# Attention and feed-forward on one core: weight sums behind the last split, PSUM quarters summed in place, Strassen from tile 8

## The chip, the cores and the metric

The kernel runs on one NeuronCore of a Trainium2 chip. The metric is the device time in microseconds of one execution; lower is better. The engines are TensorE (PE; its weight loads are shown apart as PEld), VectorE (DVE), ScalarE (ACT), GpSimd (POOL) and the queue that issues the DMAs (SP). Each works through its own instructions in order.

## What is computed

Sliding-window attention, plain for four heads and dilated by four for the other four, then a normalised feed-forward with a residual:

```python
x = attention(q, k, v)                      # B=8, H=8, S=576, D=64; window 32, dilation 4
x = x.transpose(0, 2, 1, 3).reshape(8, 576, 512)
mu, var = mean(x), mean((x - mu) ** 2)
xn = (x - mu) / sqrt(var + 1e-6) * g_ln
return x + maximum(xn @ w_ch1, 0) @ w_ch2   # w_ch1: 512 x 2048, w_ch2: 2048 x 512
```

The weights arrive as float64. Each float32 operand of a large product is split into two float16 halves, a high one (a rounded copy) and a low one (the rest), and a product is three products of halves: high x high, high x low, low x high.

## The kernel before

The 8 x 576 rows are 36 tiles of 128 rows. For each tile t the program records units of work: L (loads), S (scores), M (softmax), V (values), N (norm, and the halves for the transposes), T (two DMA transposes into xT). At the start stand the units of the weights: C and W (load and convert w1 and w2, L530 to L544), s and P (split into halves, L132 and L133). Every unit has a due time from a hand-written table (TIMES, and ORDER for the pairs); units are recorded by that time, and a scheduler then sets each engine's order by simulated durations, with the recording order as priority. `tc.high_priority()` lifts what stands under it; `tc.issue_after(i)` puts what stands under it behind instruction i.

The first FIRST tiles go through the feed-forward plainly: four up products of 512 columns a tile (`up_plain`, L344, 192 matmuls), the rectified halves (L351, L352), and a down product (`down_plain`, L363, 48 matmuls of 512 columns). All later tiles go in pairs of 256 rows through a Strassen scheme (Winograd's form): seven products where eight quarters would be multiplied. A half s (of two) of the feed-forward's columns takes seven up products (L418, 24 matmuls each) and seven down products (L487, 12 matmuls each), in the order 1, 5, 6, 2, 3, 7, 4 of their numbers. Product 1 starts the bank "u", to which 6, 7 and 4 add; 5 starts "f", to which 3 adds; 2 has "e". Between the additions `copied` takes a bank's state to SBUF (ACT L435). ORDER writes the sequence of a pair: "U06" is up product 6 of half 0, "D" a down product, "V1" and "S0" the next pair's attention, "N01" and "N05" the next pair's first two up products.

The four quarters of a half are A11, A12, A22 and A21; `added` sums a bank and a copy (DVE L440), rectifies (ACT L441), and `halves` makes a high half (ACT L426) and a low half (POOL L427). A21 is z21 (ACT L473). `summed` makes S1 = A21 + A22, S3 = A11 - A21, S2 = S1 - A11 and S4 = A12 - S2 on VectorE (L445), all operands in SBUF, and their halves. After a down product, `to_x` adds the bank into x (DVE L498); the next product into the same bank waits for it.

Strassen also needs sums of the weights, T1 to T4, for 2 weight matrices x 4 column groups: `combine` makes them in f32 (L390 to L397), then a high half (ACT L399) and a low half (L400). T1 and T2 are made on POOL, T3 and T4 on VectorE. T4 replaces a piece of the plain weights, so its halves are written after the last plain tile.

The pool z has 8 f32 buffers (NZ) for copies and sums, h has 12 for halves, ps_f has 6 PSUM banks; a buffer is given out in turn, and its next user waits until its last reader is done. The norm of a tile is: statistics (DVE L271, after the four DMAs x<-xd of L264), a power on POOL (L276), the normalised x (DVE L290), for a pair's second tile four sums (POOL L300), the halves (ACT L308, POOL L309), the transposes (L324).

Of the kernel before, what the change touches and what calls it, by code (L numbers as in the profile page):

```python
# [59 lines left out]
def attention_then_ffn(ctx: ExitStack, tc, qkv, masks, g, w1, w2, out):  # L60
    nc = tc.nc
# [68 lines left out]

    def split(src, scale, hi, lo):
        nc.scalar.activation(hi, src, AF.Copy, scale=scale)  # L132
        nc.vector.scalar_tensor_tensor(  # L133
            out=lo, in0=src, scalar=scale, in1=hi, op0=ALU.mult, op1=ALU.subtract
        )
# [247 lines left out]
    def combine(w, op, fg):  # L383
        sub, add = ALU.subtract, ALU.add
        x, y = {"T1": ("12", "11"), "T2": ("22", None), "T3": ("22", "12"), "T4": ("21", "T2")}[op]
        e = nc.vector if op in ("T3", "T4") else nc.gpsimd
        (xh, xl) = piece(w, x, fg)
        if y is None:
            z = state.pop(("T1", w, fg))
            e.tensor_tensor(out=z, in0=xh, in1=z, op=sub)  # L390
            e.tensor_tensor(out=z, in0=z, in1=xl, op=add)
        else:
            yh, yl = piece(w, y, fg)
            z = f32_tile().rearrange("p (c f) -> p c f", c=2)
            e.tensor_tensor(out=z, in0=xh, in1=yh, op=sub)
            e.tensor_tensor(out=z, in0=z, in1=xl, op=add)
            e.tensor_tensor(out=z, in0=z, in1=yl, op=sub)  # L397
        hi, lo = piece(w, op, fg)
        nc.scalar.copy(hi, z)  # L399
        e.tensor_tensor(out=lo, in0=z, in1=hi, op=sub)  # L400
        if op == "T1":
            state["T1", w, fg] = z
# [7 lines left out]
    def up_product(n, s, to, start):  # L410
        x, w = PRODUCTS[n]
        q = QUARTER[x]
        for j in range(HG):
            fc = slice(j % 2 * P, (j % 2 + 1) * P)
            ws = piece(0, w, 2 * s + j // 2)
            for k in range(2):
                for m, (l, r) in enumerate(triple([a[:, k, fc] for a in ws], (xT_pair[:, 0, q, k], xT_pair[:, 1, q, k]))):
                    nc.tensor.matmul(  # L418
                        to[:, j * P : (j + 1) * P], l, r, start=start and j == 0 and k == 0 and m == 0,
                        stop=j == HG - 1 and k == 1 and m == 2, skip_group_check=not start,  # L420
                    )

    def halves(name, me, z):
        h = me[name] = halves_tile()
        hh, hl = flat(h)
        nc.scalar.copy(hh, z)  # L426
        nc.gpsimd.tensor_tensor(out=hl, in0=z, in1=hh, op=ALU.subtract)  # L427

    def up(n, s, t0):
        me = state.setdefault(("s", t0, s), {})  # L430

        def copied(x):
            z = f32_tile()
            with tc.high_priority():
                nc.scalar.copy(z, x)  # L435
            return z

        def added(x, z, name):
            with tc.high_priority():
                nc.vector.tensor_tensor(out=z, in0=x, in1=z, op=ALU.add)  # L440
            nc.scalar.activation(z, z, AF.Relu)  # L441
            halves(name, me, z)

        def summed(to, x, y, op, name):
            nc.vector.tensor_tensor(out=me[to], in0=me[x], in1=me[y], op=op)  # L445
            halves(name, me, me[to])

        if n == 1:
            me["u"] = bank()
            up_product(1, s, me["u"], True)  # L450
            me["z11"] = copied(me["u"])
        elif n == 5:
            me["f"] = bank()
            up_product(5, s, me["f"], True)
            me["z22"] = copied(me["f"])
        elif n == 6:
            up_product(6, s, me["u"], False)
            me["z12"] = copied(me["u"])
        elif n == 2:
            e = bank()  # L460
            up_product(2, s, e, True)
            added(e, me["z11"], "A11")
        elif n == 3:
            up_product(3, s, me["f"], False)
            added(me["f"], me["z12"], "A12")
        elif n == 7:
            up_product(7, s, me["u"], False)
            added(me["u"], me["z22"], "A22")
        else:
            up_product(4, s, me["u"], False)  # L470
            me["z21"] = f32_tile()
            with tc.high_priority():
                nc.scalar.activation(me["z21"], me["u"], AF.Relu)  # L473
# [310 lines left out]
```

## Time and profile before

| | |
|---|---|
| median of 3 runs | 958.19 us (956.5 to 958.92) |
| profiled execution | 956.94 us, its span 955.1 us |
| busy share of the span: PE, DVE, POOL, ACT | 86%, 63%, 55%, 40% |
| weights arrive and are converted, first tiles | 0 to 132 us |
| plain tiles, from the first down product | 132 to 260.5 us |
| 15 pairs by Strassen | 260.5 to 955.1 us |
| mean granted TensorE clock | 0.973 of full speed |

A matmul is pipelined, so a busy PE is not PE at its peak. In the rows of the profile "out<-in" are the program's names, "x12" a count; a releaser is what ended an engine's idle time. w_sb are the weights' halves, w_sums the raw weights at first and T1 to T3 later.

### The profile page before, as it was taken

The numbers are of one execution on the slowest core, as the hardware profiler recorded it, in microseconds if no ns is written. First come the engines' busy times: TensorE is split into PE (matmuls) and PEld (weight loads), VectorE is DVE, ScalarE is ACT, GpSimd is POOL, SyncE is SP. The second block draws the span as 40 slices with busy tenths as digits, with TensorE's granted clock in tenths as the row PEclk, the third lists the DMA queues.
The fourth block names the chain that finished last, engine by engine and source line by source line (L and its number), as shares of the span: only waits on it lengthen the run. The fifth ranks groups of instructions, "written<-read, shape, count | busy, mean of one in ns | idle before, by whom it ended". The sixth has DMA issues, their size and how long they took to land.

```text
span 955.1 us, 36608 instructions
## 1 busy us (share of the span) xinstructions
PE 822.5 (86%) x16592; PEld 727.2 (76%) x16592; DVE 604.8 (63%) x1021; ACT 377.6 (40%) x624; POOL 522.1 (55%) x451
## 2 busy tenths in 40 slices
PE   3318799956999999989999899988999898898998
PEld 2218765753798988888988899887888798787897
DVE  5998663698655757474748383828473837374834
ACT  4343361220352625252534344434253425353442
POOL 2153055595356657474848483838283827374844
PEclk9999799977999999999999999999999999999999
DMA  9833523301323232323332323232324142322020
GB/s 335 301 104 132 80 65 89 69 29 34 96 75 84 78 79 77 91 62 95 80 84 71 96 58 96 58 96 57 107 46 96 45 108 58 77 66 57 19 52 24
DMA packets 118236, 81.84 MB, mean 86 GB/s; under 512 B 67840, under 2 KB 100160, under 8 KB 118080
## 3 DMA queue, kind: packets, MB, share of 16 engines
q1 hardware_dynamic: 118080, 79.50, 30.7%
q8 instruction: 130, 2.13, 0.9%
q14 instruction: 26, 0.21, 0.1%
HBM read 49.97 MB, written 9.44 MB: 62 GB/s over the span
## 4 chain that ended last, share of the span: by engine, by line
PE 39%; DVE 17%; POOL 16%; issue 12%; DMA 11%; ACT 3%; SPq 3%; DVEq 0%; POOLq 0%; ACTq 0%
PE ps_f L418 18%; PE ps_f L487 10%; POOL h L427 8%; DMA xT<-xh 4%; DMA x<-xd 3%; PE ps_a L247 3%; PE ps_f L344 3%; DVE z L445 3%; PE ps_f L363 2%; SPq L264 2%; DVE w_sb L133 2%; DMA xT<-xl 2%; POOL xl L309 2%; POOL xs L300 2%; DVE w_sums L533 1%
## 5 line engine op out<-in xcount | busy, mean ns | idle before, releaser
L427 POOL TENSOR_TENSOR h<-z,h 128x512 f16<-128x512 f32 x210 | 273.2, 1325 | 211.1 <-ACT h L426 189.8
L487 PEld LDWEIGHTS <-h 128*128 128x128 f16 x2520 | 244.1, 98 | 46.8 <-issue 17.3
L418 PE MATMUL ps_f<-xT,w_sb 128*128 128x128 f16 x2880 | 185.1, 219 | 3.3 <-issue 1.6
L418 PEld LDWEIGHTS <-w_sb 128*128 128x128 f16 x2880 | 167.8, 98 | 18.6 <-issue 13.5
L487 PE MATMUL ps_f<-w_sb,h 128*128 128x256 f16 x1440 | 174.2, 274 | 0.6 <-DVE x L498 0.6
L426 ACT CAST h<-z 128x512 f16<-128x512 f32 x210 | 127.7, 618 | 93.0 <-DVE z L445 89.7
L418 PE MATMUL ps_f<-xT,w_sums 128*128 128x128 f16 x2160 | 138.3, 220 | 22.8 <-DMA xT<-xh 8.9
L498 DVE SCALAR_TENSOR_TENSOR x<-ps_f,s,x 128x256 f32<-128x256 f32 x210 | 94.6, 472 | 94.9 <-PE ps_f L487 94.4
L445 DVE TENSOR_TENSOR z<-z 128x512 f32<-128x512 f32 x120 | 134.1, 1118 | 21.4 <-ACT z L473 16.9
L487 PE MATMUL ps_f<-w_sums,h 128*128 128x256 f16 x1080 | 134.5, 275 | 14.9 <-DVE x L498 14.0
L418 PEld LDWEIGHTS <-w_sums 128*128 128x128 f16 x2160 | 126.7, 98 | 15.6 <-issue 15.2
L435 ACT COPY z<-ps_f 128x512 f32<-128x512 f32 x90 | 52.5, 585 | 142.9 <-PE ps_f L418 142.9
L440 DVE TENSOR_TENSOR z<-ps_f,z 128x512 f32<-128x512 f32 x90 | 60.5, 684 | 57.5 <-PE ps_f L418 56.1
L344 PE MATMUL ps_f<-xT,w_sb 128*128 128x128 f16 x1152 | 70.9, 226 | 23.1 <-DMA xT<-xh 18.4
L344 PEld LDWEIGHTS <-w_sb 128*128 128x128 f16 x1152 | 69.2, 102 | 24.9 <-issue 22.7
L309 POOL TENSOR_TENSOR xl<-xs,xh 128x512 f16<-128x512 f32 (+1 forms) x36 | 67.1, 1863 | 38.2 <-ACT xh L308 33.3
L441 ACT ACTIVATE z<-z 128x512 f32<-128x512 f32 x90 | 56.2, 628 | 44.1 <-DVE z L440 44.1
L247 PE MATMUL ps_a<-v_prev,pt 32*32 32x65 f32 x1152 | 49.3, 234 | 16.0 <-DVE pt L225 8.4
L308 ACT CAST xh<-xs 128x512 f16<-128x512 f32 (+1 forms) x36 | 31.8, 884 | 76.6 <-DVE xs L290 36.2
L271 DVE BATCH_NORM_STATS2 bs<-x 128x6 f32<-128x512 f32 x36 | 24.9, 691 | 55.3 <-DMA x<-xd 54.6
L276 POOL TENSOR_TENSOR rstd<-rstd,mhalf 128x1 f32<-128x1 f32 x36 | 20.5, 571 | 70.0 <-DVE rstd L275 66.4
L193 PE MATMUL ps_a<-ks,q 64*32 64x64 f32 (+1 forms) x2976 | 43.3, 220 | 16.7 <-issue 15.8
(89 smaller groups left out, 923.0 us busy)
## 6 DMA issues: line engine op xcount, KB each, us to landing
w_sums<-in_w SPq DMA_DIRECT2D x14, 1024.0 KB, 10.1
ks<-in_qkv SPq DMA_DIRECT2D x36, 256.0 KB, 3.3
q<-in_qkv SPq DMA_DIRECT2D x36, 256.0 KB, 3.5
vs<-in_qkv SPq DMA_DIRECT2D x36, 256.0 KB, 4.1
out_x<-x SPq DMA_DIRECT2D x36, 256.0 KB, 2.0
x<-xd SPq DMA_DIRECT2D x144, 32.0 KB, 2.3
v_prev<-in_qkv SPq DMA_DIRECT2D x35, 128.0 KB, 2.7
w_sums<-in_w SPq DMA_DIRECT2D x4, 512.0 KB
```

Of the source, the lines that this page charges most:

```text
L247: nc.tensor.matmul(pv[to, b, g, e], pt[pj, b, h, n], v[pj, f, e], start=n == 0 or b == 1 and old is None, stop=n == 1,)
L309: nc.gpsimd.tensor_tensor(out=xl[:, 0:m], in0=x, in1=xh[:, 0:m], op=ALU.subtract)
L344: nc.tensor.matmul(z[:, n * P : (n + 1) * P], l, r, start=n == 0 and c == 0 and m == 0, stop=n == HG - 1 and c == NKC - 1 and m == 2,)
L418: nc.tensor.matmul(to[:, j * P : (j + 1) * P], l, r, start=start and j == 0 and k == 0 and m == 0, stop=j == HG - 1 and k == 1 and m == 2, ...
L426: nc.scalar.copy(hh, z)
L427: nc.gpsimd.tensor_tensor(out=hl, in0=z, in1=hh, op=ALU.subtract)
L435: nc.scalar.copy(z, x)
L440: nc.vector.tensor_tensor(out=z, in0=x, in1=z, op=ALU.add)
L441: nc.scalar.activation(z, z, AF.Relu)
L445: nc.vector.tensor_tensor(out=me[to], in0=me[x], in1=me[y], op=op)
L487: nc.tensor.matmul(to[:, 0:KQ], l, r, start=start and j == 0 and m == 0, stop=j == HG - 1 and m == 2, skip_group_check=not start,)
L498: nc.vector.scalar_tensor_tensor(out=x, in0=ps[:, 0:KQ], scalar=state["inv"], in1=x, op0=ALU.mult, op1=ALU.add)
```

## The change

- `combine` runs wholly on VectorE, and its instructions are placed behind the last recorded split. T2 and T4 of w2 take other signs.
- A11 and A12 stay in PSUM: `added` adds the copy into the bank (new L449), ScalarE rectifies from there into the high half (new L435), VectorE makes the low half in one instruction (new L436). `summed` rectifies as it reads the bank (new L458), for S2, S4 and S3; S1 alone has both operands in SBUF (new L456). S1, S2 and S4 each take a new buffer of z. S2 has the opposite sign.
- FIRST is 8, with due times for tiles 6 and 7: 14 pairs are left.
- Tile 0's S, M, V, N and T are recorded at high priority.

```diff
-FIRST = 6
+FIRST = 8
...
+SOON = ("S0", "M0", "V0", "N0", "T0")
...
-        nc.vector.scalar_tensor_tensor(
+        state["split"] = nc.vector.scalar_tensor_tensor(
...
-        e = nc.vector if op in ("T3", "T4") else nc.gpsimd
...
+        e = nc.vector
+        with tc.issue_after(state["split"]):
+            if op == "T2":
+                z = state.pop(("T1", w, fg))
+                xh, xl = piece(w, "22", fg)
+                if w:
+                    terms = (z, xh, sub), (z, xl, sub)
+                else:
+                    terms = (xh, z, sub), (z, xl, add)
+            else:
...
+                terms = (xh, yh, minus), (z, xl, add), (z, yl, minus)
+            for a, b, by in terms:
+                e.tensor_tensor(out=z, in0=a, in1=b, op=by)
...
-    def halves(name, me, z):
+    def halves(name, me, z, plain=True):
...
+        nc.scalar.activation(hh, z, AF.Relu)
+        return nc.vector.scalar_tensor_tensor(out=hl, in0=z, scalar=0.0, in1=hh, op0=ALU.max, op1=ALU.subtract).ins
...
-                nc.vector.tensor_tensor(out=z, in0=x, in1=z, op=ALU.add)
-            nc.scalar.activation(z, z, AF.Relu)
-            halves(name, me, z)
+                nc.vector.tensor_tensor(out=x, in0=x, in1=z, op=ALU.add)
+            me["after", name] = halves(name, me, x, False)
...
+                    nc.vector.scalar_tensor_tensor(out=to, in0=x, scalar=0.0, in1=y, op0=ALU.max, op1=op)
...
-            summed("s", "z21", "z22", ALU.add, "S1")
-            summed("z21", "z11", "z21", ALU.subtract, "S3")
-            summed("z11", "s", "z11", ALU.subtract, "S2")
-            summed("z12", "z12", "z11", ALU.subtract, "S4")
+            s1 = summed("S1", z21, me["p5"], ALU.add)
+            s2 = summed("S2", me["e"], s1, ALU.subtract, me["after", "A11"])
+            summed("S4", me["f"], s2, ALU.add, me["after", "A12"])
+            summed("S3", me["e"], z21, ALU.subtract, me["after", "A11"], z21)
...
+        with tc.high_priority() if name in SOON else nullcontext():
+            what()
```

The change moves instructions on every engine. The new file's line numbers are higher, by 1 at the start and by 17 in the later parts (new L515 is L498). On the DMA queue, where tile 1 is transposed, stood:

```order
L264 DMA x<-xd 32x256 x4
L526 DMA w_sums<-in_w 128x2x1024
L152 DMA q<-in_qkv 128x512
L526 DMA w_sums<-in_w 128x2x1024 x2
L151 DMA ks<-in_qkv 128x512
L324 DMA_TRANSPOSE xT<-xh_538 128x4x128
L324 DMA_TRANSPOSE xT<-xl_539 128x4x128
```

and now, on the same queue:

```order
L265 DMA x<-xd 32x256 x4
L543 DMA w_sums<-in_w 128x2x1024
L153 DMA q<-in_qkv 128x512
L325 DMA_TRANSPOSE xT<-xh_538 128x4x128
L325 DMA_TRANSPOSE xT<-xl_539 128x4x128
L543 DMA w_sums<-in_w 128x2x1024 x2
L152 DMA ks<-in_qkv 128x512
```

Tile 1's two transposes stand ahead of the last two loads of w2 and no longer behind them.

On VectorE, in the second half of a pair, from the add of two down products to the second tile's norm, stood (of the pairs two forms occur; this one has the statistics early):

```order
L498 SCALAR_TENSOR_TENSOR x<-ps_f,s_1703,x 128x256 x2
L252 TENSOR_SCALAR rs<-ps_a 128x8
L253 RECIPROCAL rs<-rs 128x8
L257 TENSOR_TENSOR x<-ps_a,rs 128x256
L257 TENSOR_TENSOR xd<-ps_a,rs 128x256
L445 TENSOR_TENSOR z<-z 128x512 x2
L271 BN_STATS bs<-x 128x6
L445 TENSOR_TENSOR z<-z 128x512
L498 SCALAR_TENSOR_TENSOR x<-ps_f,s_1703,x 128x256
L273 BN_AGGR mv<-bs 128x2
L445 TENSOR_TENSOR z<-z 128x512
L275 TENSOR_SCALAR rstd<-mv 128x1
```

and now, on VectorE at the same place:

```order
L515 SCALAR_TENSOR_TENSOR x<-ps_f,s_1703,x 128x256 x2
L253 TENSOR_SCALAR rs<-ps_a 128x8
L254 RECIPROCAL rs<-rs 128x8
L258 TENSOR_TENSOR x<-ps_a,rs 128x256
L258 TENSOR_TENSOR xd<-ps_a,rs 128x256
L456 TENSOR_TENSOR z<-z 128x512
L458 SCALAR_TENSOR_TENSOR z<-ps_f,z 128x512 x2
L515 SCALAR_TENSOR_TENSOR x<-ps_f,s_1703,x 128x256
L272 BN_STATS bs<-x 128x6
L458 SCALAR_TENSOR_TENSOR z<-ps_f,z 128x512
L515 SCALAR_TENSOR_TENSOR x<-ps_f,s_1703,x 128x256
L274 BN_AGGR mv<-bs 128x2
```

The add of down product 6 (the first L515 behind the sums) stands ahead of the statistics, three of the four sums too, and the sums read PSUM.

On ScalarE, in the first half of a pair, from the copies of products 1 and 5 of half 1 on, stood:

```order
L435 COPY z<-ps_f 128x512 x2
L223 ACTIVATE sc<-sc 128x512
L473 ACTIVATE z<-ps_f 128x512
L308 CAST xh_5526<-xs 128x512
L435 COPY z<-ps_f 128x512
L426 CAST h<-z 128x512 x3
```

and now, on ScalarE at the same place:

```order
L444 COPY z<-ps_f 128x512 x2
L224 ACTIVATE sc<-sc 128x512
L491 ACTIVATE z<-ps_f 128x512
L309 CAST xh_5427<-xs 128x512
L432 CAST h<-z 128x512 x2
L444 COPY z<-ps_f 128x512
L432 CAST h<-z 128x512 x2
```

The copy of product 6 of half 1 stands behind the high halves of S1 and S2 of half 0. POOL's run of low halves ahead of the second tile's norm (L276) is 9 long, or 8 with one behind, where it was 11.

More of the change, by code (lines that the diff above doesn't have):

```diff
@@ L31 @@
 NQK = 2 * HP * P
-FIRST = 6
+FIRST = 8
 KQ = 256
 EARLY = 4
-GAP = 17.2
 SOFTMAX, VALUES, NORM, READY = 1.0, 12.0, 4.5, 4.0
@@ L46 @@
     "C": (0.0, 12.0, 30.0, 40.0), "W": (50.0, 3.2), "P": 98.0, "T": 104.0,
-    "U": (42.0, 62.0, 82.0), "D": 100.0, "t": (2.0, 22.0, 50.0, 75.0, 94.0, 118.0),
+    "U": (42.0, 62.0, 82.0), "D": 100.0, "t": (2.0, 22.0, 50.0, 75.0, 94.0, 118.0, 142.0, 165.0),
 }
+SOON = ("S0", "M0", "V0", "N0", "T0")
 MOVED = {
@@ L132, in split @@
         nc.scalar.activation(hi, src, AF.Copy, scale=scale)
-        nc.vector.scalar_tensor_tensor(
+        state["split"] = nc.vector.scalar_tensor_tensor(
             out=lo, in0=src, scalar=scale, in1=hi, op0=ALU.mult, op1=ALU.subtract
-        )
+        ).ins
     state = {}
@@ L384, in combine @@
         sub, add = ALU.subtract, ALU.add
-        x, y = {"T1": ("12", "11"), "T2": ("22", None), "T3": ("22", "12"), "T4": ("21", "T2")}[op]
-        e = nc.vector if op in ("T3", "T4") else nc.gpsimd
[L387 to L402, printed above, removed]
+        e = nc.vector
[8 more added lines that the diff above has]
+            else:
+                x, y = {"T1": ("12", "11"), "T3": ("22", "12"), "T4": ("21", "T2")}[op]
+                minus = add if w and op == "T4" else sub
+                (xh, xl), (yh, yl) = piece(w, x, fg), piece(w, y, fg)
+                z = f32_tile().rearrange("p (c f) -> p c f", c=2)
+                terms = (xh, yh, minus), (z, xl, add), (z, yl, minus)
+            for a, b, by in terms:
+                e.tensor_tensor(out=z, in0=a, in1=b, op=by)
+            hi, lo = piece(w, op, fg)
+            nc.scalar.copy(hi, z)
+            e.tensor_tensor(out=lo, in0=z, in1=hi, op=sub)
+            if op == "T1":
+                state["T1", w, fg] = z
     PRODUCTS = {
@@ L421, in up_product @@
                     )
-    def halves(name, me, z):
+    def halves(name, me, z, plain=True):
         h = me[name] = halves_tile()
         hh, hl = flat(h)
-        nc.scalar.copy(hh, z)
-        nc.gpsimd.tensor_tensor(out=hl, in0=z, in1=hh, op=ALU.subtract)
+        if plain:
+            nc.scalar.copy(hh, z)
+            nc.gpsimd.tensor_tensor(out=hl, in0=z, in1=hh, op=ALU.subtract)
+            return None
+        nc.scalar.activation(hh, z, AF.Relu)
+        return nc.vector.scalar_tensor_tensor(out=hl, in0=z, scalar=0.0, in1=hh, op0=ALU.max, op1=ALU.subtract).ins
     def up(n, s, t0):
@@ L439, in added, with summed @@
             with tc.high_priority():
-                nc.vector.tensor_tensor(out=z, in0=x, in1=z, op=ALU.add)
-            nc.scalar.activation(z, z, AF.Relu)
-            halves(name, me, z)
-        def summed(to, x, y, op, name):
-            nc.vector.tensor_tensor(out=me[to], in0=me[x], in1=me[y], op=op)
-            halves(name, me, me[to])
+                nc.vector.tensor_tensor(out=x, in0=x, in1=z, op=ALU.add)
+            me["after", name] = halves(name, me, x, False)
+        def summed(name, x, y, op, behind=None, to=None):
+            to = f32_tile() if to is None else to
+            with nullcontext() if behind is None else tc.issue_after(behind):
+                if behind is None:
+                    nc.vector.tensor_tensor(out=to, in0=x, in1=y, op=op)
+                else:
+                    nc.vector.scalar_tensor_tensor(out=to, in0=x, scalar=0.0, in1=y, op0=ALU.max, op1=op)
+            halves(name, me, to)
+            return to
         if n == 1:
@@ L450, in up @@
             up_product(1, s, me["u"], True)
-            me["z11"] = copied(me["u"])
+            me["p1"] = copied(me["u"])
         elif n == 5:
@@ L710, in attention_then_ffn @@
             attention_of_pair(t + 2, name)
-    for _, _, what in sorted(units.values(), key=lambda e: e[:2]):
-        what()
+    for name, (_, _, what) in sorted(units.items(), key=lambda e: e[1][:2]):
+        with tc.high_priority() if name in SOON else nullcontext():
+            what()
 def _masks():
```

23 lines of the change are left out of this document (13 added, 10 removed).

## The prediction

> **What bounds the kernel now.** I read the page's first lines, then a table of stretches cut where the work changes character, then the waits of TensorE, then the chain of waits.
>
> ```profile
> span 955.1 us, 36608 instructions
> PE 822.5 (86%) x16592; PEld 727.2 (76%) x16592; DVE 604.8 (63%) x1021; ACT 377.6 (40%) x624; POOL 522.1 (55%) x451
> ```
>
> TensorE (PE) is busy for 86%, so at most 133 us of waiting can go, unless its work shrinks. The table of stretches says where (us; after each engine's name its busy time):
>
> ```profile
> core 0: us, PE busy (x) PEld busy (x) DVE busy (x) ACT busy (x) POOL busy (x), PEclk, DMA share, GB/s
> 20.00:84.00 64.00, 22.84 (x458) 20.45 (x448) 64.00 (x90) 25.57 (x38) 24.64 (x14) 1.00 0.51 178
> 84.00:132.00 48.00, 39.15 (x975) 37.39 (x972) 36.91 (x66) 25.74 (x45) 4.29 (x5) 0.86 0.49 120
> 132.00:179.00 47.00, 46.87 (x750) 28.89 (x748) 15.31 (x35) 9.95 (x18) 24.65 (x24) 1.00 0.28 78
> 179.00:223.00 44.00, 24.64 (x410) 18.45 (x398) 43.93 (x40) 9.34 (x17) 44.00 (x29) 0.79 0.15 34
> 223.00:260.50 37.50, 37.25 (x561) 23.90 (x562) 28.42 (x46) 10.28 (x17) 12.48 (x12) 0.93 0.31 79
> 260.50:909.50 649.00, 605.22 (x12753) 555.59 (x12752) 387.32 (x696) 271.96 (x447) 389.17 (x334) 0.99 0.29 74
> ```
>
> Two stretches belong to VectorE: 20 to 84 (64.00 of 64 us busy) and 179 to 223 (43.93 of 44, with POOL at 44.00 too). From 260.5 on TensorE leads with small waits. Those, from 290 to 909:
>
> ```profile
> PE ps_f L487 <- DVE x L498: 14.0, 12, 2.7
> PE ps_f L418 <- DMA xT<-xl: 8.6, 5, 2.7
> PE ps_f L418 <- DMA xT<-xh: 7.6, 8, 2.4
> ```
>
> L498 adds a down product into x and so frees its bank for the next product; xT are the transposed inputs of a pair's second tile. The chain of waits gives landmarks (start, length):
>
> ```profile
> 91.00 10.85 DMA xT<-xh
> 101.89 10.09 PE ps_f L344 x145
> 209.27 13.98 issue
> 224.49 12.48 PE ps_f L363 x48
> 239.65 1.41 PE ps_a L247 x91
> 241.06 8.15 PE ps_f L344 x144
> 250.17 10.47 PE ps_f L363 x48
> 260.64 5.36 PE ps_f L418 x96
> 301.91 3.40 DMA xT<-xh
> 346.41 3.45 DMA xT<-xh
> 910.20 3.38 DMA xT<-xh
> ```
>
> The transposes at 301.91 and 910.20 serve pairs 2 and 15: 608.3 / 13 = 46.8 us a pair, and 44.5 where it goes well (301.91 to 346.41). From the first Strassen product (260.5) to pair 2's transposes are 41.4 us, from pair 15's to the end 44.9.
>
> **Weight sums leave the start (first part).** VectorE's groups from 20 to 90 us, and the spread of two lines (min/median/max ns):
>
> ```profile
> L133 DVE SCALAR_TENSOR_TENSOR w_sb<-w_sb,gs 128x512 f16<-128x512 f32 x12 | 13.1, 1110 | 0.0
> L395 DVE TENSOR_TENSOR z<-w_sb 128x512 f32<-128x512 f16 x4 | 5.6, 1399 | 0.0
> L397 DVE TENSOR_TENSOR z<-z,w_sb 128x512 f32<-128x512 f32 x4 | 3.6, 898 | 0.0
> L396 DVE TENSOR_TENSOR z<-z,w_sb 128x512 f32<-128x512 f32 x4 | 2.7, 676 | 0.0
> L133 DVE SCALAR_TENSOR_TENSOR w_sb<-w_sb,gs x12: 692/745/1654, 19.8 to 72.4; 128x512 f16<-128x512 f32 x12
> L396 DVE TENSOR_TENSOR z<-z,w_sb x16: 655/1036/1646, 28.7 to 238.3; 128x512 f32<-128x512 f32 x16
> ```
>
> The new wait on the last split takes 12 sums out of VectorE's full stretch: 5.6 + 3.6 + 2.7 = 11.9 us. POOL's sums go as well, and with them the doubled durations: L133's 12 splits took 13.1 us against 12 x 0.745 = 8.9, so 4.2 us more. Together 16 us. Third, the order puts tile 1's transposes ahead of the last two loads of w2; they took 10.85 us behind them and 3.40 in a quiet queue: up to 7 us. "First tile first" adds little: in the order its norm stands as before, between the same splits. The first down product now starts at 132.0 (the table's cut). I take 22 us of the 16 + 7, so 110; bounds 121 (only the 11.9 count) and 105 (more follows).
>
> **Two more plain tiles.** From there to the first Strassen product TensorE has 8 x 48 down products at 10.47 / 48 = 0.218 us (83.8), 5 x 192 up products at 8.15 / 144 = 0.0566 (54.3), and six tiles' attention, values at 1.41 and scores at about 1.2 (an estimate, near the values; 15.7): 154 us. Beside it VectorE does all 120 sums. Their price, bounded by L396: 0.655 alone, 1.646 against POOL. At 0.655 they are 79 us. VectorE's other work from 132 to 260.5 was its 87.7 busy us (15.31 + 43.93 + 28.42) less 48 sums at some 1.2, about 30; with two more tiles about 40 (both estimates). 119 fit into 154, but not at every point, since VectorE works in order, and behind a sum stand the softmax transposes that the value products wait for and the low halves that the down products wait for. I add 13 us of waits (bounds 0 and 40). First Strassen product: 110 + 154 + 13 = 277 (before 260.5), with one pair fewer to come.
>
> [...]
>
> **The pairs' stage.** The page's groups (count, busy us, mean ns):
>
> ```profile
> L427 POOL TENSOR_TENSOR h<-z,h 128x512 f16<-128x512 f32 x210 | 273.2, 1325 | 211.1 <-ACT h L426 189.8
> L445 DVE TENSOR_TENSOR z<-z 128x512 f32<-128x512 f32 x120 | 134.1, 1118 | 21.4 <-ACT z L473 16.9
> L440 DVE TENSOR_TENSOR z<-ps_f,z 128x512 f32<-128x512 f32 x90 | 60.5, 684 | 57.5 <-PE ps_f L418 56.1
> ```
>
> Per pair POOL loses 4 of 14 low halves (5.3 us), ScalarE four copies. VectorE had 6 x 0.684 + 8 x 1.118 = 13.0 us; now 16 with a PSUM operand and 2 sums of SBUF operands, 16 x 0.684 + 2 x 1.118 = 13.2. The form that writes PSUM in place is unseen; its bounds are L440 (0.684) and L445 (1.118), and I take 0.684 since it reads the same operands. So no engine's sum limits; the waits do, and the order and one good pair show them:
>
> ```profile
> 324.96 15.06 POOL L427 TENSOR_TENSOR h<-z,h 128x512 f16<-128x512 f32 x11 [1.34 <-PE ps_f L418]
> 323.30 0.57 ACT L435 COPY z<-ps_f 128x512 f32<-128x512 f32 x1
> 323.58 3.09 DVE L445 TENSOR_TENSOR z<-z 128x512 f32<-128x512 f32 x3
> 324.79 1.50 PE L418 MATMUL ps_f<-xT,w_sums 128*128 128x128 f16 x24
> 327.44 1.47 PE L487 MATMUL ps_f<-w_sums,h 128*128 128x256 f16 x12
> DVE bs L271 <- DMA x<-xd: 54.6, 24, 8.4
> ```
>
> - Product 6 of down frees its bank now ahead of the norm statistics (L271), which wait for a DMA; before, in some pairs, behind them. The 14.0 us of waits on L498, 1.0 a pair, go.
> - The second tile's norm stands on POOL behind 9 low halves and not 11 (2 x 1.37 us from 15.06 / 11), and the sums ahead of it are shorter. Of the 16.2 us waiting for xT (1.2 a pair) I take 0.8; the good pair keeps some wait too, so not all.
> - New: seven f32 buffers a half and not five, of eight. The copy of product 6 now stands on ScalarE behind the copies of S1 and S2, and product 7 into the same bank (324.79) waits for it. The sums start at 323.58: two of them (1.4), the cast of the second and the copy (0.6 each) end about 326.1, 1.3 us late, of which nine products of down 1 moved ahead cover 1.0. I take 0.4 (bounds 0 and 1.3).
> - Two banks are held until S4 and S3 are read; at 0.684 a sum S4, the third, is read by about 325.7, ahead of 327.44. Cost nothing; its cover is those 1.7 us.
> - Clock. A stretch with a wait of 2.7 us:
>
> ```profile
> 620.00:640.00 20.00, 16.83 (x399) 15.67 (x398) 6.23 (x14) 6.07 (x10) 4.84 (x3) 0.91 0.36 86
> ```
>
> 0.91 of full speed over 20 us is 1.8 us lost. The stage's 0.99 is some 6.5 us, 0.46 a pair, and I take 0.3 of it with the waits. [...]
>
> A pair: 46.8 - 1.0 - 0.8 - 0.3 + 0.4 = 45.1 (bounds 44.2, all waits and clock gone, and 48.1, only the new one).
>
> **The sum.** 277 + 41 + 12 x 45.1 + 44.9 = 904 us of span. The profiled execution took 956.94 us for 955.1 of span, so 906. The runs' median, 958.19, is 0.13% above that execution.
>
> **Rivals.**
> 1. The pairs stay at 46.8: what the copy and the statistics hold back eats the gain. 906 + 12 x 1.7 = 926. For it: 54.6 us of waits on xd stay.
> 2. VectorE's queue binds the start: waits of 40 and not 13, 933 us. For it: 179 to 223 shows what such sums do to TensorE. Against: POOL is free of them.
> 3. All goes well: pairs 44.2, waits 5, first down product at 105: 906 - 11 - 8 - 5 = 882.
> 4. Slower than before: the held banks. If the first tile's statistics come late by the longest wait, 8.4 us, S4 is late and the down product that takes its bank waits 8.4 - 1.7 = 6.7 us: 906 + 12 x 6.7 = 986. It decides from (957 - 906) / 12 = 4.2 us a pair; the mean wait, 54.6 / 24 = 2.3, is far below.
>
> **Chances.** Forecast 0.50, rivals 0.17, 0.12, 0.15 and 0.06. The range reaches over rivals 1 to 3, 878 to 934; the forecast's own is 893 to 919. Faster by over 0.3% (about what a measurement can tell from no change) 0.93, within 0.01, slower 0.06.
>
> **What would show it.** The profile after should have the first down product near 110, VectorE without its contended sums before that, the first Strassen product near 277 with waits on softmax transposes and low halves, no wait of a down product on the add into x over 1 us, and transposes of a pair 45 us apart. I am wrong if VectorE stays full past 160 while TensorE idles, or if products 7 or down 5 wait several us for a copy or a bank.

## The result, and the profile after

| | before | after |
|---|---|---|
| median of 4 runs | 957.35 us (956.41 to 958.92) | 911.21 us (908.87 to 913.51) |
| ratio | | 0.952, 95% interval 0.948 to 0.955 |
| span of the profiled execution | 955.1 us | 907.9 us |

Forecast were 906 us. One of the six executions of a later kernel, h3_same_pairs, took 1372.66 us at a granted clock of 0.577 and is left out of that kernel's numbers. The page of the new kernel begins:

```profile
span 907.9 us, 36333 instructions
PE 820.7 (90%) x16568; PEld 718.6 (79%) x16568; DVE 578.9 (64%) x1115; ACT 329.7 (36%) x548; POOL 326.7 (36%) x321
```

TensorE works about as long as before (820.7 us, before 822.5); 45 of the 47 us are waits that went. The table of stretches, cut as before and with the pairs' stage behind (after each engine's name its busy time, then the granted clock):

```profile
20.00:84.00 64.00, 32.53 (x720) 29.45 (x708) 57.49 (x96) 30.05 (x51) 4.24 (x4) 0.97 0.68 225
84.00:132.00 48.00, 46.29 (x784) 36.16 (x783) 42.58 (x75) 21.73 (x34) 3.44 (x3) 0.97 0.24 70
132.00:179.00 47.00, 41.24 (x734) 27.39 (x732) 34.96 (x66) 11.46 (x20) 7.15 (x7) 0.93 0.27 75
179.00:223.00 44.00, 41.44 (x666) 31.39 (x665) 44.00 (x76) 11.01 (x19) 8.57 (x4) 1.00 0.15 44
223.00:260.50 37.50, 34.06 (x724) 24.99 (x723) 13.14 (x29) 5.29 (x9) 6.56 (x7) 0.95 0.36 90
302.98:842.82 539.84, 517.03 (x11041) 474.39 (x11041) 319.04 (x650) 203.99 (x336) 255.03 (x241) 1.00 0.31 79
```

From 20 to 84 us VectorE has 6.5 us to spare where it had none, and TensorE does 32.53 us of work instead of 22.84. From 179 to 223 VectorE is full again, 37 of its 44 us with sums and their low halves, now without POOL's sums beside it, and TensorE goes on (41.44 of 44; before 24.64). Two landmarks, TensorE's first down product (L364) and its first Strassen product (L423):

```profile
114.78 1.04 PE L364 MATMUL ps_f<-w_sb,h 128*128 128x512 f16 x4
282.34 5.38 PE ps_f L423 x96
```

They cut the span in three: the start 114.8 us (before 132.0), the plain tiles 167.4 (before, with two tiles fewer, 128.5), the pairs 625.7 (before, with one pair more, 694.6). TensorE's waits in the pairs' stage from 290 to 862 (us in all, times, longest):

```profile
PE ps_f L423 <- DMA xT<-xh: 5.6, 6, 1.9
PE ps_f L423 <- ACT z L444: 4.0, 9, 0.9
PE ps_f L423 <- DMA xT<-xl: 3.9, 4, 1.5
PE ps_f L504 <- DVE x L515: 3.0, 5, 0.8
```

And from the page's groups POOL's low halves and the new sum in PSUM (count, busy us, mean ns):

```profile
L433 POOL TENSOR_TENSOR h<-z,h 128x512 f16<-128x512 f32 x140 | 159.1, 1157 | 263.5 <-ACT h L432 260.7
L449 DVE TENSOR_TENSOR ps_f<-ps_f,z 128x512 f32<-128x512 f32 x56 | 37.7, 693 | 46.6 <-PE ps_f L423 46.3
```

The wait on the add into x is 3.0 us (14.0 before, on the old L498), that on the transposes 9.5 (16.2), that on the copies 4.0. The sum in PSUM takes 0.693 us. POOL's low halves got shorter on average, 1.157 us against 1.325, with no change to them.

### The profile page after: what moved, and what is told of

It is laid out like the page before. It is cut to its first block, busy times and chain, and to the rows that moved or that the text cites. A ratio compares the mean times of both kernels' runs of the same rounds, so it can differ in the third digit from the quotient of the medians.

```text
span 907.9 us, 36333 instructions
## 1 busy us (share of the span) xinstructions
PE 820.7 (90%) x16568; PEld 718.6 (79%) x16568; DVE 578.9 (64%) x1115; ACT 329.7 (36%) x548; POOL 326.7 (36%) x321
## 4 chain that ended last, share of the span: by engine, by line
PE 48%; DVE 13%; DMA 10%; issue 6%; POOL 5%; SPq 4%; ACT 3%; DVEq 0%; POOLq 0%; ACTq 0%
PE ps_f L423 16%; PE ps_f L504 14%; PE ps_f L364 7%; DMA x<-xd 6%; PE ps_f L345 5%; PE ps_a L248 4%; SPq L265 4%; DVE z L402 3%; DMA xT<-xl 2%; POOL xs L301 2%; DMA xT<-xh 2%; DVE xs L291 2%; PE ps_a L194 2%; DVE z L458 1%; POOL xl L310 1%
## 5 line engine op out<-in xcount | busy, mean ns | idle before, releaser
L433 POOL TENSOR_TENSOR h<-z,h 128x512 f16<-128x512 f32 x140 | 159.1, 1157 | 263.5 <-ACT h L432 260.7
L504 PEld LDWEIGHTS <-h 128*128 128x128 f16 x2352 | 224.9, 98 | 32.3 <-issue 5.8
L423 PE MATMUL ps_f<-xT,w_sb 128*128 128x128 f16 x2688 | 173.5, 219 | 2.2 <-issue 2.1
L423 PEld LDWEIGHTS <-w_sb 128*128 128x128 f16 x2688 | 156.3, 98 | 17.1 <-issue 12.6
L504 PE MATMUL ps_f<-w_sb,h 128*128 128x256 f16 x1344 | 162.7, 273 | 0.7 <-DVE x L515 0.6
L423 PE MATMUL ps_f<-xT,w_sums 128*128 128x128 f16 x2016 | 128.1, 219 | 16.4 <-DMA xT<-xh 7.5
L515 DVE SCALAR_TENSOR_TENSOR x<-ps_f,s,x 128x256 f32<-128x256 f32 x196 | 89.8, 475 | 82.4 <-PE ps_f L504 81.9
L423 PEld LDWEIGHTS <-w_sums 128*128 128x128 f16 x2016 | 117.4, 98 | 11.9 <-issue 11.5
L345 PE MATMUL ps_f<-xT,w_sb 128*128 128x128 f16 x1536 | 95.3, 226 | 13.9 <-DMA xT<-xh 11.7
L345 PEld LDWEIGHTS <-w_sb 128*128 128x128 f16 x1536 | 92.6, 102 | 16.9 <-issue 15.0
L432 ACT CAST h<-z 128x512 f16<-128x512 f32 x140 | 83.8, 617 | 50.7 <-DVE z L458 26.5
L444 ACT COPY z<-ps_f 128x512 f32<-128x512 f32 x84 | 49.0, 584 | 124.6 <-PE ps_f L423 124.6
L364 PE MATMUL ps_f<-w_sb,h 128*128 128x512 f16 x336 | 74.1, 379 | 1.3 <-DVE h L353 1.3
L223 POOL TENSOR_TENSOR sc<-sc,mx 128x512 f32<-128x512 f32 x32 | 39.9, 1247 | 93.8 <-DVE mx L211 81.3
L449 DVE TENSOR_TENSOR ps_f<-ps_f,z 128x512 f32<-128x512 f32 x56 | 37.7, 693 | 46.6 <-PE ps_f L423 46.3
L364 PEld LDWEIGHTS <-h 128*128 128x128 f16 x336 | 32.2, 98 | 39.5 <-DVE h L353 1.5
L248 PEld LDWEIGHTS ps_a<-v_prev,pt 32*32 32x32 f32 x1152 | 39.2, 108 | 22.1 <-issue 20.2
```

The lines of the kernel that those rows point to most:

```text
L223: nc.gpsimd.tensor_tensor(out=sc, in0=sc, in1=mx.broadcast_to([P, 2, HP, 2 * W]), op=ALU.subtract)
L248: nc.tensor.matmul(pv[to, b, g, e], pt[pj, b, h, n], v[pj, f, e], start=n == 0 or b == 1 and old is None, stop=n == 1,)
L345: nc.tensor.matmul(z[:, n * P : (n + 1) * P], l, r, start=n == 0 and c == 0 and m == 0, stop=n == HG - 1 and c == NKC - 1 and m == 2,)
L364: nc.tensor.matmul(o, l, r, start=part == 0 and n == 0 and m == 0, stop=part == 3 and n == HG - 1 and m == 2,)
L423: nc.tensor.matmul(to[:, j * P : (j + 1) * P], l, r, start=start and j == 0 and k == 0 and m == 0, stop=j == HG - 1 and k == 1 and m == 2, ...
L449: nc.vector.tensor_tensor(out=x, in0=x, in1=z, op=ALU.add)
```

## The experiments

Each is the new kernel with the edit shown. "Start" ends at the first down product, "plain" at the first Strassen product, "pairs" at the end; all from the profiled execution.

| kernel | start | plain | pairs | median, us | ratio to before (95%) |
|---|---|---|---|---|---|
| before | 132.0 | 128.5 | 694.6 (15 pairs) | 957.35 | 1 |
| after | 114.8 | 167.4 | 625.7 | 911.21 | 0.952 (0.948 to 0.955) |
| e5_not_soon | 120.1 | 166.8 | 622.8 | 909.68 | 0.948 (0.944 to 0.953) |
| e1_sums_free | 134.3 | 164.5 | 626.7 | 924.09 | 0.963 (0.960 to 0.967) |
| e2_pool_sums | 121.0 | 180.4 | 628.5 | 930.1 | 0.969 (0.966 to 0.972) |
| e3_first6 | 114.8 | 116.1 | 680.3 (15 pairs) | 914.61 | 0.954 (0.949 to 0.959) |
| e4_old_pairs | 119.4 | 168.1 | 638.9 | 928.83 | 0.968 (0.964 to 0.972) |
| f1_nz9 | 115.8 | 166.9 | 623.0 | 911.25 | 0.952 (0.949 to 0.955) |
| f3_w2_loads_first | 120.6 | 163.1 | 622.3 | 908.29 | 0.949 (0.945 to 0.952) |
| f4_softmax_first | 116.5 | 163.0 | 629.6 | 909.74 | 0.951 (0.947 to 0.954) |
| g4_stats_behind | 120.3 | 158.9 | 629.2 | 905.92 | 0.945 (0.942 to 0.948) |
| g2_order | 117.6 | 167.0 | 628.0 | 914.38 | 0.954 (0.950 to 0.958) |
| g5_both | 117.5 | 157.0 | 625.7 | 903.9 | 0.943 (0.940 to 0.946) |
| h3_same_pairs | 117.7 | 164.1 | 623.8 | 905.26 | 0.943 (0.938 to 0.948) |

The start spreads by itself: e5_not_soon differs from the new kernel by four small matmuls' places and starts its down products 5.3 us later. All kernels here but e1, e2 and f3 have the new kernel's order on VectorE up to the last split and no sums on POOL, and their starts run from 114.8 to 120.3. The totals of one kernel spread by 4 to 9 us from execution to execution, so two medians of the table that are less than about 5 us apart are not told from each other. The stages come from one execution of each kernel.

**First tile first** (e5_not_soon).

```diff
-SOON = ("S0", "M0", "V0", "N0", "T0")
+SOON = ()
```

> The new kernel without the high priority of tile 0's units; in the order only four score matmuls of TensorE move. Theory (this part does nothing): first down product at 114 to 121, the spread that equal orders showed, 909 to 914 us. Rival (tile 0's earlier scores start VectorE's softmax earlier and carry through): 916 us or more.

909.68 us: no effect is seen, as expected. This kernel also serves as a second measurement of the new one: 909.7 and 911.2.

**The wait on the last split** (e1_sums_free).

```diff
-        with tc.issue_after(state["split"]):
+        with nullcontext():
```

> The new kernel, but its weight sums don't wait for the last split; all stay on VectorE. In the order 28 of them now stand ahead of the last split, and the last three loads of w2 stand ahead of tile 1's transposes again. My theory (VectorE's queue is the start's bound, each sum in it costs its time): 28 x 0.68 = 19 us more in VectorE's start, of which its 6.5 idle us from 20 to 84 take some, and the transposes land later by up to 4: first down product at 125 to 132 (114.85 in the new kernel), some 6 us of it given back behind it since fewer sums are left there; 919 to 925 us. Rival (only the contention with POOL cost something in the start; without POOL the sums fit beside the rest): first down product by 118, L134's splits still at 0.74, 909 to 914 us.

924.09 us, 13 to 14 us slower, with the start at 134.3, a little later than expected. (The edit also puts loads of w2 ahead of tile 1's transposes again; f3_w2_loads_first below shows that this alone costs nothing.) VectorE is full from 20 to 84 again:

```profile
20.00:84.00 64.00, 29.91 (x568) 27.33 (x557) 64.00 (x109) 29.25 (x43) 4.68 (x2) 1.00 0.63 227
84.00:132.00 48.00, 30.73 (x653) 28.90 (x653) 43.54 (x74) 25.95 (x47) 5.69 (x4) 0.75 0.17 45
```

The groups of VectorE from 20 to 134 have 44 sums and low halves; of the largest group:

```profile
L402 DVE TENSOR_TENSOR z<-z,w_sb 128x512 f32<-128x512 f32 x20 | 13.4, 679 | 0.0
```

The sums run at 0.68 us with POOL out of the way, and still cost their time: VectorE's queue is the start's bound, and not only the contention with POOL. Behind it TensorE is idle for a third of 84 to 132, at a clock of 0.75. Only 3 us came back in the plain tiles, not the 6 expected.

**T1 and T2 on POOL again** (e2_pool_sums).

```diff
-        e = nc.vector
+        e = nc.vector if op in ("T3", "T4") else nc.gpsimd
```

> The new kernel with T1 and T2 made on POOL again, behind the last split as now. My theory (sums on both engines slow each other, and softmax on POOL queues behind them): the start stays (first down product at 114 to 116), the sums on VectorE take 1.0 us and more at the median instead of 0.68, and the plain tiles' stage grows from 167.5 by 10 us (0 to 25): 921 us (911 to 936). Rival (VectorE's in-order queue alone was the cost, and 56 instructions fewer in it relieve it): the stage shrinks to some 160, 903 us.

930.1 us: 19 to 20 us slower. The plain tiles take 180.4, 13 more. VectorE has 56 instructions fewer, but the 64 that are left take 1.17 us on average beside POOL instead of 0.72, and the value products wait 15.5 us at one place for a softmax transpose (L226); the kernel before had a wait of 5.6 us of this kind. The spread of VectorE's largest group of sums (min/median/max ns):

```profile
L402 DVE TENSOR_TENSOR z<-z,w_sb x24: 676/1538/1643, 123.6 to 229.7; 128x512 f32<-128x512 f32 x24
```

TensorE's waits from 121 to 301, and the stretch from 179:

```profile
PE ps_a L248 <- DVE pt L226: 15.5, 1, 15.5
```

```profile
179.00:223.00 44.00, 27.30 (x375) 20.34 (x374) 41.32 (x46) 9.18 (x16) 36.88 (x27) 0.77 0.10 31
```

The rival, that relief for VectorE's queue would win, is out. One part of the expectation missed: the start is 121.0, not 114 to 116. Most of that is within the spread of equal orders; a part is that the placement behind a split held VectorE's sums but not the first three of POOL's. They show the contention by itself. Rows of POOL and VectorE (start, length); in the new kernel the three splits took 2.07 us and L554 1.22, so the two rows are 2.8 us longer here:

```profile
25.01 3.09 POOL L402 TENSOR_TENSOR z<-z,w_sb 128x512 f32<-128x512 f32 x2 [0.70 <-DVE w_sb L134]
...
23.21 3.88 DVE L134 SCALAR_TENSOR_TENSOR w_sb<-w_sb,gs 128x512 f16<-128x512 f32 x3
27.01 2.17 DVE L554 SCALAR_TENSOR_TENSOR w_sb<-w_sums 128x1024 int32<-128x1024 int32 x1
```

**Strassen from tile 6** (e3_first6).

```diff
-FIRST = 8
+FIRST = 6
```

> The new kernel with FIRST = 6, so that 15 pairs run; all else as it is. My theory: a pair of plain tiles has 47.9 us of work for TensorE (2 x (10.47 + 10.86 + 2.6)), a Strassen pair takes 45.0, so the trade itself costs 3 us, and two more tiles pay only as cover for the 120 sums. With six tiles (106 us of work) the sums (82 us) and VectorE's other 30 no longer fit: waits of 20 to 25 instead of 13.5, first Strassen product at 241 to 246, and 911.2 - 41 + 45 = 915 us (908 to 922). Rival A (the cover isn't needed, waits stay 13.5): 234 and 908 us, faster than the new kernel. Rival B (the tiles are most of the gain, the queue binds): 260 and 933 us.

914.61 us, and the theory said 915. Its place was wrong: the plain tiles took 116.1 us and not 126 to 131, with waits of 7.4 in them. The other waits came directly behind, at the first Strassen products (length of the wait in brackets):

```profile
230.87 0.22 PE L423 MATMUL ps_f<-xT,w_sb 128*128 128x128 f16 x1 [1.84 <-DMA xT<-xh]
239.87 0.28 PE L248 MATMUL ps_a<-v_prev,pt 32*32 32x65 f32 x1 [6.21 <-issue]
246.92 0.37 PE L423 MATMUL ps_f<-xT,w_sums 128*128 128x128 f16 x2 [4.99 <-DMA xT<-xh]
```

VectorE's sums run to 229 us and hold up the norm and softmax of the first pair. 7.4 and 13.0 are the 20 us of waits that were expected, against 11.8 with eight plain tiles. So the two tiles are cover for the sums. What they are worth in total, 3 to 5 us, is no more than what these runs can tell from nothing.

**The pairs' sums in SBUF again** (e4_old_pairs; `halves`, `added` and `summed` as before, T2 and T4 of w2 in their old signs).

```diff
-                nc.vector.tensor_tensor(out=x, in0=x, in1=z, op=ALU.add)
-            me["after", name] = halves(name, me, x, False)
+                nc.vector.tensor_tensor(out=z, in0=x, in1=z, op=ALU.add)
+            nc.scalar.activation(z, z, AF.Relu)
+            halves(name, me, z)
```

> The new kernel, but the pairs' quarters and their sums S1 to S4 as before the change (all in SBUF, S2, T2 and T4 in their old signs). My theory: start and plain tiles stay (first Strassen product at 282), a pair goes back from 45.0 to 46.8 us, mostly through waits on the add into x and on the second tile's transposes: 911.2 + 13 x 1.8 = 935 us (930 to 938). Rival (the pairs run better because of something else, for instance no weight sums beside the first ones, or where the tiles' attention falls): 45.0 a pair stays, 909 to 914 us.

928.83 us, 18 to 19 slower. Of these 13 to 16 lie in the pairs' stage (638.9 against 625.7 and 622.8), the rest in the start, which the edit doesn't touch. It is less than the 23 us expected. VectorE's sums and POOL's low halves are slow again, and TensorE's waits on transposes and the add are back (groups, then waits, in the pairs' stage):

```profile
L447 DVE TENSOR_TENSOR z<-z 128x512 f32<-128x512 f32 x103 | 114.2, 1109 | 14.5 <-ACT z L475 12.9
...
L429 POOL TENSOR_TENSOR h<-z,h 128x512 f16<-128x512 f32 x178 | 231.2, 1323 | 162.3 <-ACT h L428 159.5 <-PE ps_f L489 1.3
```

```profile
PE ps_f L420 <- DMA xT<-xl: 12.9, 9, 2.5
PE ps_f L489 <- DVE x L500: 9.7, 14, 1.2
```

The longest wait on the add is 1.2 us here and was 2.7 in the kernel before. There the statistics stood ahead of that add in three of 13 pairs, with 14 pairs they do so in none. The pairs are also 9 us shorter here than 14 pairs of the kernel before (694.6 less one pair of 46.8), with the old sums in both. So a part of the gain in the pairs did not come with the PSUM quarters. The new order of the pairs is the likely cause; no run tests it alone.

**The copy of product 6** (f1_nz9, then g2_order).

```diff
-NH, NZ, NX = 12, 8, 5
+NH, NZ, NX = 12, 9, 4
```

> The new kernel with nine f32 buffers (NZ) instead of eight and four x buffers (NX) instead of five to make room. Theory (the copy of product 6 waits on ScalarE behind the high halves of S1 and S2 because the eight buffers are out): TensorE's waits on the copies (L444), 4.0 us from 290 to 862, go to nearly nothing and the kernel gains 2 to 5 us: 907 us (905 to 910). Rival (the products only wait for the next thing, the second tile's transposes, or the scheduler moves other work in front): 910 to 914 us, and the waits on xT grow by what the copies' lose.

No gain (911.25 us), and the waits on the copies stay: 3.9 us in place of 4.0. With nine buffers the copy keeps its place on ScalarE, so my reason for that place, that the buffers are out, is wrong. ScalarE's rows of the new kernel show what holds the copy (L444): it stands behind the high halves of S1 and S2 (L432). Product 6 itself was done at 342.4.

```profile
344.83 1.34 ACT L432 CAST h<-z 128x512 f16<-128x512 f32 x2 [0.57 <-DVE z L456]
346.08 0.58 ACT L444 COPY z<-ps_f 128x512 f32<-128x512 f32 x1
```

```diff
-"U13", "U17", "D01", "D05",
+"U13", "D01", "U17", "D05",
```

> The new kernel with one change in ORDER: down product 1 of half 0 goes whole (12 matmuls, not 9) ahead of up product 7 of half 1. f1_nz9 showed that more buffers don't take the wait on the copies away (3.9 us of L444 from 290 to 862). Theory (the copy of product 6 is late because ScalarE makes S1's and S2's high halves first, in its order, whatever the buffers; three more matmuls, 0.33 us, cover that much of each wait): waits on L444 2 us or less, 0 to 4 us gained: 908 us (906 to 911). Rival (the sequence behind shifts as well, and D5 or the norm is late instead): 911 to 915 us.

The wait went down, the time didn't:

```profile
PE ps_f L423 <- ACT z L444: 1.5, 4, 0.8
```

914.38 us, not told from the new kernel: 2.5 us of waits went at this place, and other waits of the pairs' stage took theirs (gaps of TensorE from the first Strassen product on: 26.0 us, 25.9 in the new kernel).

**Tile 1's transposes behind the loads of w2** (f3_w2_loads_first).

```diff
-    "L0": -3.3, "L1": 10.2, "W4": 48.5, "W6": 65.8,
+    "L0": -3.3, "L1": 10.2, "W4": 48.5, "W6": 65.8, "T1": 76.0,
```

> The new kernel, but tile 1's two transposes stand behind the last two loads of w2 on the DMA queue, as before the change; its sums stay behind the last split. Theory (the loads in front cost the transposes up to 7 us of landing): tile 1's first up product moves from 80.6 to some 84 to 87, the first down product from 114.8 to 117 to 120, 915 us (912 to 918). Rival (the loads come earlier by as much, and with them the last split and tile 2, so nothing is lost): first down product at 112 to 115, 908 to 912 us.

908.29 us: nothing is lost. Tile 1's first up product moved from 80.6 to 89.3, more than expected, but the first down product is at 120.6, at the late end of the spread of equal orders, and the plain tiles are 4 us shorter. The rival is nearer, though the first down product did not come early as it said.

**What the plain tiles wait for** (f4_softmax_first, g4_stats_behind, h3_same_pairs). VectorE's and TensorE's rows of the new kernel around its longest wait there:

```profile
147.83 0.41 DVE L258 TENSOR_TENSOR xd<-ps_a,rs 128x256 f32<-128x256 f32 x1
153.34 0.69 DVE L272 BATCH_NORM_STATS2 bs<-x 128x6 f32<-128x512 f32 x1 [5.09 <-DMA x<-xd]
...
155.63 0.68 DVE L202 TENSOR_TENSOR sc<-ps_a,mask 128x512 f32<-128x512 f32 x1
...
160.19 0.28 PE L248 MATMUL ps_a<-v_prev,pt 32*32 32x65 f32 x1 [4.54 <-issue]
```

VectorE is not busy with sums here. It is idle for 5.09 us at one tile's statistics, which need four DMAs, and the next tile's softmax (from L202 on) is queued behind them. The trace calls TensorE's wait "issue"; VectorE's rows show what it is. The first try moved due times only: those of loads, scores and softmax of tiles 5 to 8, by 10 us and more.

> The new kernel with earlier due times for loads, scores and softmax of tiles 5 to 8 alone: in the order VectorE's mask add of tile 5 (L202) now stands ahead of tile 4's statistics (L272), which wait for a DMA. Theory (in the plain tiles TensorE's two longest waits, 4.5 us at 155.7 and 3.4 us at 236.4, come from VectorE sitting idle at L272 for x<-xd with the next softmax queued behind it, and not from the sums): both waits shrink below 1.5 us, the slow clock behind them (0.93 and 0.95) goes, and the kernel gains 6 to 13 us: 902 us (898 to 905). Rival (the sums bind: VectorE is full from 179 to 223, and what is put ahead there pushes the rest back): the waits move, 908 to 915 us.

One of the two waits shrank (3.4 to 1.1 us), the other (4.4) stayed, since in the order its statistics still stood in front. Plain tiles 163.0, and the pairs took 4 us more: 909.74. The second try puts the order down:

```diff
-        nc.vector.bn_stats(bs, x)
+        late = state[t + 1].get("softmax") if 3 <= t < FIRST and t + 1 in state else None
+        with nullcontext() if late is None else tc.issue_after(late):
+            nc.vector.bn_stats(bs, x)
```

> As f4_softmax_first, with tile 4 earlier too, and the statistics of tiles 3 to 7 (L274 in this file) placed on VectorE behind the next tile's softmax transposes (L226) by a wait of their own, since due times alone left the statistics of the fifth tile in front. Theory (VectorE idle at the statistics with the next softmax behind them makes TensorE's waits of 4.4 and 3.4 us in the plain tiles): no wait of the value products over 1.5 us from 132 to 260, no slow clock there, plain tiles' stage at 156 to 160 instead of 163 to 167, 903 us (900 to 906). Rival (the norm comes late in its turn, the transposes of the next tile arrive late and TensorE waits for xT instead, or the pairs give it back): stage at 163 or more, 908 to 912 us.

The plain tiles take 158.9 us, 8.5 fewer, and the stretch with the long wait runs at full clock:

```profile
132.00:179.00 47.00, 45.80 (x763) 28.69 (x762) 39.19 (x74) 14.19 (x25) 12.15 (x7) 1.00 0.29 75
```

VectorE's idle time at the statistics from 114 to 283 is 2.3 us (14.2 in the new kernel). TensorE's waits in the plain tiles fall from 11.8 to 4.3 us with it. That shows the mechanism. Of the 8.5 us some 4 are lost in the pairs again (629.2) in the profiled execution, which with 910.21 us is the slowest of this kernel's six. With the order of g2_order added:

> The statistics of g4_stats_behind and the order of g2_order together. Theory: the two gains lie in different stages and add up: 901 us (897 to 905). Rival (neither carries through): 908 to 912 us.

903.9 us, the lowest median of all, 6 to 7 us under the new kernel (0.943, interval 0.940 to 0.946; the new kernel's two measurements 0.952 from 0.948, and 0.948 from 0.944). It is not told from g4_stats_behind (0.945), and g2_order had no gain to add. Is the loss in the pairs due to their order? In the traces f4_softmax_first and g4_stats_behind have one and the same order of VectorE's 731 rows from the first in-place add on, and it is not that of the new kernel; the last kernel has the new kernel's.

```diff
-        late = state[t + 1].get("softmax") if 3 <= t < FIRST and t + 1 in state else None
+        late = state[t + 1].get("softmax") if t in (3, 4, 7) and t + 1 in state else None
```

> As g4_stats_behind, but only where the two long waits were: the statistics of tiles 3, 4 and 7 stand behind the next tile's softmax transposes, and only tiles 4, 5 and 8 have earlier due times. In the order VectorE's rows from the first in-place add on are the same 731 as the new kernel's; in g4_stats_behind and f4_softmax_first 546 of them stood elsewhere, and there the pairs' stage took 629 us and not 623 to 626. Theory (the pairs gave back some 4 us only because the scheduler ordered them anew): plain tiles' stage 157 to 161 us, pairs' stage 622 to 626, 902 us (899 to 904). Rival (the pairs' stage is longer because of what the plain tiles leave, whatever the order): 628 us or more for it, 906 to 909.

The pairs' stage is 623.8, as the theory said: with this order it took 622.8 to 625.7 in three kernels, with that of f4_softmax_first and g4_stats_behind 629.6 and 629.2. That fits a loss by order, with one execution of each. The plain tiles were 164.1, which the theory didn't say. A wait of 4.0 us now stands at 184.8, and this one is made by the sums, on POOL: the softmax's subtraction (L223) takes 5.03 us beside them, 1.04 where VectorE runs none (the row ahead of it).

```profile
152.96 1.04 POOL L223 TENSOR_TENSOR sc<-sc,mx 128x512 f32<-128x512 f32 x1 [3.29 <-DVE mx L211]
180.29 5.03 POOL L223 TENSOR_TENSOR sc<-sc,mx 128x512 f32<-128x512 f32 x1 [4.33 <-DVE mx L211]
```

905.26 us, the same as g4_stats_behind. Nearest to having both is g5_both, with 157.0 and 625.7.

## Why the prediction was right, point by point

**The sum.** Forecast were a start of 110, plain tiles of 167 and 627 from there; measured 114.8, 167.4 and 625.7. The terms are near for partly other reasons than given.

**The start: mechanism right, size 5 to 10 us too large.** The 16 us of sums and contention hold: L133's successor (L134) takes 0.742 us on average instead of 1.110, VectorE has room, and giving 28 sums back costs 13 us in all (e1_sums_free). (The bound of 121 should read 120, 132.0 less 11.9.) The step that failed is the third, up to 7 us from the order of the DMAs, of which I took 6. Landing did get shorter (10.85 to 6.2 us, not 3.4), and tile 1's first up product comes 8.7 us earlier than without it (f3_w2_loads_first), but undoing it cost nothing in the total. That the loads which now come later hold up what follows is a guess; no run shows it. Where TensorE begins to run through, at tile 1's first up product, the gain is 21.3 us (101.89 to 80.64); 4 of them are gone by the first down product, since the value products of two tiles instead of one stand between.

**Two more plain tiles: size right, reason half wrong.** 154 us of work and 13 of waits were forecast, and TensorE's gaps are 11.8. The sums cost a little more than was taken: 0.68 us at the median against 0.655, and 86.5 us for all 120 against 79, since four took 1.2 to 2.7. The step that failed is what the waits come from: I had the softmax and the low halves wait behind sums. The two longest waits, 4.5 and 3.4 us, are VectorE idle at statistics that wait for a DMA (g4_stats_behind). Sums did make one of 4.0 us in h3_same_pairs, and there not by their place in VectorE's queue but through POOL, whose subtraction took 5.03 us beside them and 1.04 without. That the tiles serve as cover is shown by e3_first6 (20 us of waits instead of 11.8); what they pay in total it can't tell from nothing.

**The pairs: 45.1 forecast, 45.07 measured.** The transposes of a pair's second tile are issued at

```profile
322.02 1.34 SPq L325 DMA_TRANSPOSE xT<-xh  x1
...
862.81 2.24 SPq L325 DMA_TRANSPOSE xT<-xh  x1
```

with 12 pairs between: 540.79 / 12. By terms: the add gives 0.8 (14.0 / 13 less 3.0 / 12; forecast 1.0), the transposes 0.5 (16.2 / 13 less 9.5 / 12; forecast 0.8), and the clock is 1.00. The new wait on the copy costs 0.1 (4.0 / 12 against 3.4 / 13; forecast 0.4), and its reason was wrong: f1_nz9. The remaining 0.5 is about what the clock of 0.99 had cost (0.46). Undone alone, the PSUM quarters are worth 13 to 16 us; the other 9 or so came with something else, which the prediction did not separate and e4_old_pairs shows without naming it. That 45.07 meets 45.1 so closely is in part luck: the four terms were off by 0.2 to 0.3 us each and cancel. The in-place add is 0.693 us (taken 0.684), S1 with both operands in SBUF 0.691 at the median (taken 1.118), and the held banks cost nothing, as taken.

**The rivals.** Pairs at 46.8: no. VectorE's queue with waits of 40: no; even with POOL's sums beside it TensorE's gaps are 23.4 us (e2_pool_sums). All well: only the pairs came near (45.07, not 44.2). Held banks: no wait of a down product on a sum appears.

**The contention and the clock.** The sums that read a bank take 0.68 us, those of e4_old_pairs with both operands in SBUF 1.109. In the plain tiles the sums of weights, both operands in SBUF, kept their 0.68 at the median beside POOL's softmax, and POOL paid: up to 5.04 us for a subtraction that took 1.04 where VectorE ran no sums (last section).

The clock: in the new kernel it halves 2.6 us into the wait of 4.5 us and 0.4 us behind that of 3.4, and in the pairs, with waits up to 1.9, it is 1.00. In the pairs of the kernel before it halves at four waits of 2.2 to 2.7 us, and at one of 2.7 it stays 1.00 (at 425.7); the last section has the idle time around them.

## What to carry to other kernels

When an engine is full in a stage, move its work to a stage that has cover, and count the cover at each point of its queue: the longest waits here were made not by the moved work but by an instruction that waited for a DMA at the head of an in-order queue, with the next tile's work behind it. Read the waiting engine's rows, not its busy share: 34.96 of 47 us busy hid a wait of 5 us that TensorE paid for. And judge an edit by the stage it touches: where due times alone changed the scheduler's order elsewhere, that stage was some 4 us longer.

## What the runs showed of the hardware that I had not expected

- A POOL instruction took several us longer beside a run of VectorE sums, up to where VectorE came to an instruction that reads a bank. The softmax's subtraction, 128 x 512, took 1.04 us in the plain tiles of the new kernel where VectorE ran no sums, and 3.23 and 5.04 where it ran one sum with both operands in SBUF after the other:

```profile
130.27 3.23 POOL L223 TENSOR_TENSOR sc<-sc,mx 128x512 f32<-128x512 f32 x1 [31.15 <-DVE mx L211]
...
157.64 1.04 POOL L223 TENSOR_TENSOR sc<-sc,mx 128x512 f32<-128x512 f32 x1
179.54 5.04 POOL L223 TENSOR_TENSOR sc<-sc,mx 128x512 f32<-128x512 f32 x1 [4.33 <-DVE mx L211]
...
183.00 0.68 DVE L405 TENSOR_TENSOR w_sums<-z,w_sums 128x512 f16<-128x512 f32 x1
183.60 0.74 DVE L369 SCALAR_TENSOR_TENSOR x<-ps_f,s,x 128x512 f32<-128x512 f32 x1
```

L369 reads a bank. POOL's second long subtraction ends at 184.58, 0.98 us behind the start of L369, about what it needs alone. So it seems to have done next to nothing in the 4 us of sums ahead (an estimate from these times). The one of 3.23 us ends at 133.50, 0.99 us behind the start of an L369 at 132.51, and that of 5.03 us in h3_same_pairs at 185.32, 0.98 us behind the same add (there L371) at 184.34. Whether placing such an instruction among the sums earlier would free POOL was not tried.

- POOL's low halves in the pairs took 1.157 us on average instead of 1.325 once most of VectorE's sums there read PSUM, and 1.323 with the old sums back (e4_old_pairs).
- The clock halved after short waits as well. From 130 us on it does so six times in the profile of the kernel before and twice in that of the new one, and the stretches at half clock are 3.41, 6.83 or 17.07 us long: once, twice or five times the shortest. In the 3.41 us ahead of these eight changes TensorE was idle for 2.07 to 3.01 us. Cut into steps of that length from one of the changes on, the two traces have no step with more than 1.92 us of idle time and full clock behind it; in the kernel before these 1.92 are a part of the wait of 2.69 us at 425.74. So some 2 us of a step were enough in these two kernels (an estimate from these figures). That step and one ahead of a change, each with the step behind it, and the last of the new kernel's changes (the clock is the third figure from the end):

```profile
426.51:429.92 3.41, 1.49 (x22) 1.16 (x29) 3.38 (x7) 1.24 (x2) 2.13 (x2) 1.00 0.01 2
429.92:433.34 3.42, 3.42 (x93) 3.06 (x94) 2.71 (x4) 0.00 (x0) 2.98 (x5) 1.00 0.37 95
624.49:627.90 3.41, 1.26 (x15) 1.00 (x13) 0.00 (x0) 0.00 (x0) 0.00 (x0) 1.00 0.82 162
627.90:631.31 3.41, 2.84 (x26) 2.71 (x26) 0.00 (x0) 0.19 (x1) 0.00 (x0) 0.50 0.04 16
```

```profile
236.79:240.20 3.41, 0.41 (x41) 0.44 (x44) 2.29 (x4) 2.04 (x4) 2.15 (x2) 1.00 0.61 181
240.20:243.61 3.41, 3.41 (x122) 3.24 (x113) 1.19 (x5) 0.00 (x0) 0.00 (x0) 0.50 0.49 112
```

In g4_stats_behind less idle time was followed by a slow clock: 1.49 us from 234 to 238, and a clock of 0.57 from 238 to 242. What made the difference there no run separates.

```profile
234.00:238.00 4.00, 2.51 (x145) 2.17 (x143) 1.67 (x5) 1.22 (x2) 1.70 (x2) 1.00 0.38 125
238.00:242.00 4.00, 4.00 (x44) 4.00 (x44) 1.12 (x4) 0.19 (x1) 0.00 (x1) 0.57 0.74 143
```

- The start varies by 5 us (114.8 to 120.3) between kernels that have one and the same order on VectorE there, and the difference builds up from the first DMAs on: in e4_old_pairs the tenth load of weights is issued 1.1 us later than in the new kernel (by 26.75 and 25.65 us), the transposes that start at 97.85 in the new kernel start at 99.50, and the first down product is 4.6 us later (119.4 and 114.8).
